# Two loads for w1's first rows, first FFN products on four banks, packed turns of q: one change to a fused attention and FFN kernel

## The chip, the core and the metric

The kernel runs on one core of a Trainium2 chip. The metric is the device time of one execution in microseconds (us); the text compares medians of several runs. A profile is one further execution, recorded by the hardware profiler, with its own time.

A core has five engines that run their own instruction queues in order and wait for each other through semaphores: PE (TensorE: matrix products, results into PSUM), DVE (VectorE), ACT (ScalarE), POOL (GpSimd, used here to issue loads that also convert fp32 to bf16) and SP (SyncE, used here to issue stores and transposing transfers). PSUM has eight banks of 512 fp32 columns by 128 partitions.

## What is computed

Linformer attention for 8 batches of 8 heads (1024 positions, head size 64), followed by a feed-forward layer (FFN) with a maximum over three products:

```python
k_proj = einsum('ks,bhsd->bhkd', E, k)            # 64 projected positions
v_proj = einsum('ks,bhsd->bhkd', F, v)
scores = q @ k_proj^T / sqrt(64)
attn   = softmax(scores)
x      = (attn @ v_proj) -> 8192 tokens x 512
h      = max(x @ w1, x @ w2, x @ w3)              # 512 x 768 each
out    = h @ w_out                                # 768 x 512
```

## The kernel before

**Tiling.** A batch is a loop turn `b` of eight. Its 1024 tokens are two chunks `ch` of 512. The 512 model columns are four row blocks `ct` of the weights (128 rows each; one block of x is one pair of heads, `g` or "pair"), the 768 hidden columns six blocks `jt`. Everything multiplied is bf16.

**FFN.** `up_mm` (line 565) issues one 128x128 by 128x512 product for one weight `i`, one `jt` and one `ct`. For most chunks `up` (609) does the three weights of one `jt`, ACT copies the first result (625), DVE takes the maxima (629, and `most`, 577), then `down` (655) multiplies by `w_out` for four token tiles `tt`. Steps 0 to 5 of a chunk are the `jt`, steps 6 to 9 the `tt`.

**Attention for a batch** is woven between these steps: `kproj` and `vproj` (E and F against k and v, 341 to 351), `kt` (turn of the projected keys), `qd` (380: DVE packs q into `q_p` head by head side by side, SP turns it with a transposing transfer), `sc` (321: scores; the exponentials on ACT are put off to the next `run_later` unless `now` is set), then sums and values. `za` (330) takes the sums of one pair with a matrix of ones, the values, and on ACT logarithm and exponential for the reciprocal (`invert`, 288), and DVE scales the values into `xT` (`scale_x`, 305). `zc` (248) does the sums of a whole chunk in a compact form: the reciprocals go to DRAM (`zd`, line 268, on SP) and come back spread over partitions (`zi_all`, four transfers, line 275, on SP or on the queue given).

**Order.** Everything is placed by hand. `plan(b)` (685) is a table: key `(ch, step)` gives what is issued after that step; `(1, (3, "mid"))` is in the middle of step 3. Queues keep the order of issue.

**PSUM banks** are dealt by the program when it is built. `two()` (77) gives an aligned pair and `bank()` (82) one bank; both take what is free earliest by the kernel's own arithmetic of when each engine gets there (`clock`, `free`; `at(us)` moves that arithmetic on). A bank dealt but not yet read out is marked open and isn't dealt again. If its former reader is later on the chip than assumed, PE waits.

**The start.** Loads for batch 0 are issued by POOL in lines 167 to 195: q, k and v by parts, w1's row blocks 0 and 1 as one load (185), v for pairs 2 and 3, w1's other blocks, w2, w3, the second half of q, w_out. The first chunk of batch 0 has its own attention, in lines 507 to 559: `v_pair(g)` projects v for a pair, `z(g)` does sums and reciprocals, `x(g)` values and scaling. `idle` issues products on a constant, whose results nobody reads. Then `up_first` (580) does the first FFN chunk: six banks for w1, `ct` outside and `jt` inside; `work` says what is issued after product `(0, ct, jt)`. After that, w2 and w3 (i = 1, 2) each run first with row blocks 0 and 1 (step "a"), then with 2 and 3, each followed by DVE's maximum. `qp` (363), issued within the w3 part, turns chunk two of q on PE: `heads_q` (353) turns one head of 64 columns at a time.

The next batch's q, k and v are loaded by `ld`; in batch 1's plan the loads of batch 3 stand at `(0, 3)` and `(0, 8)`.

Of the kernel before, what the change touches and what calls it, by code (L numbers as in the profile page):

```python
# [15 lines left out]
def kernel(  # L16
# [60 lines left out]
    def two():  # L77
        n = min(range(0, 8, 2), key=lambda n: max(free[n:n + 2]))
        deal((n, n + 1))
        return psum_t[:, n:n + 2, :], (n, n + 1)  # L80
# [80 lines left out]
    def load_w(i, cts):  # L161
        w = (moe_w1, moe_w2, moe_w3)[i].rearrange("(ct p) j -> p ct j", p=P)
        nc.gpsimd.dma_start(out=w_sb[i][:, cts, :], in_=w[:, cts, :])
# [18 lines left out]
            at = hp * 16 + c * 8  # L182
            nc.vector.memset(pick[c * HALF:(c + 1) * HALF, hp, at:at + 8], 1.0)

    load_w(0, slice(0, 2))
    load_kv(2, V2)
    load_kv(2, V3)
    load_w(0, slice(2, 3))
# [132 lines left out]
    def sc(b, g, lo=0, nsi=SI, now=False):  # L321
        def f():
            t = scores(b, g, lo, nsi)
            if now:
                exps(b, g, lo, nsi, t)
            else:
                later.append(lambda: exps(b, g, lo, nsi, t))
        return f

    def za(b, g, lo=0, nsi=SI, then=False):  # L330
        def f():
            z = sums(b, g, lo, nsi)
            av = values(b, g, lo, nsi)
            invert(b, g, lo, nsi, z)
            if then:
                later.append(lambda: scale_x(b, g, lo, nsi, av))
            else:
                scale_x(b, g, lo, nsi, av)
        return f
# [13 lines left out]
    def heads_q(b, g, sis, t):  # L353
        for i, si in enumerate(sis):
            for hp in range(2):
                nc.tensor.transpose(
                    out=t[hp * HALF:(hp + 1) * HALF, i * P:(i + 1) * P],
                    in_=qkv[b][0][:, 2 * g + hp, si, :],
                    identity=ident,
                )  # L360
        pe(0.08 * len(sis))

    def qp(b, gs, lo=0, nsi=SI):
        def f():
            if b not in qTs:
                qTs[b] = att.tile([P, NPAIR * SI, P], BF16, name="qT")
            t, ns = two()
            t = t.bitcast(BF16)[:, 0]
            n = nsi * P
            for i, g in enumerate(gs):  # L370
                heads_q(b, g, range(lo, lo + nsi), t[:, i * n:(i + 1) * n])
            o = qTs[b].rearrange("a (g si) p -> a g si p", si=SI)
            copy(
                "v", o[:, gs[0]:gs[-1] + 1, lo:lo + nsi, :],
                t[:, 0:len(gs) * n].rearrange("a (g si p) -> a g si p", si=nsi, p=P),
                ns, 0.1 + len(gs) * nsi * 0.08,
            )
        return f
# [20 lines left out]
    def kproj(b):  # L399
        def f():  # L400
            t, ns = bank()
            proj(b, 1, t, (LO, HI), 4 * D)
            kps[b] = att.tile([P, 2, 2 * D], BF16, name="kp")
            copy("v", kps[b].rearrange("a g x -> a (g x)"), t[:, 0:4 * D], ns, 0.43)
        return f
# [31 lines left out]
    def idle(n, w=warm):  # L437

        t, ns = bank()
        for _ in range(n):  # L440
            nc.tensor.matmul(out=t, lhsT=w[:, 0:P], rhs=w, start=True, stop=True)  # L441
        free[ns[0]] = pe(n * MM * (4 if w is warm_f else 1))
# [19 lines left out]
    def at(us):  # L462
        clock["pe"] = max(clock["pe"], us)
# [56 lines left out]
    def z(g):  # L520
        invert(0, g, *C0, sums(0, g, *C0))

    def x(g):
        scale_x(0, g, *C0, values(0, g, *C0))
# [28 lines left out]
        exps(0, g, *C0, scores(0, g, *C0))  # L553
    at(16.1)
    v_pair(1)
    idle(1)
    x(1)
    z(2)
    z(3)
    at(18.2)  # L560

    ffn_sb = ctx.enter_context(tc.tile_pool(name="ffn_sb", bufs=2))
    hTs = {}
# [16 lines left out]
    def up_first(work):  # L580


        def then(key):
            run_later()
            for f in work.get(key, []):
                f()

        hs = ffn_sb.tile([P, NJT, CHUNK], FP32, name="hs", bufs=1)
        hTs[0, 0] = ffn_sb.tile([P, NJT, CHUNK], BF16, name="hT")
        jts = range(NJT)  # L590
        h = [(t[:, n], ns[n:n + 1]) for t, ns in (two(), two(), two()) for n in (0, 1)]
        for ct in range(NCT):
            for jt in jts:
                up_mm(h[jt][0], 0, 0, 0, jt, (ct,))
                if ct == NCT - 1:
                    copy("sv"[jt % 2], hs[:, jt], *h[jt])
                then((0, ct, jt))
        for i in (1, 2):
            h = []
            for jt in jts:  # L600
                h.append(bank())
                up_mm(h[jt][0], i, 0, 0, jt, range(NCT // 2))
                then((i, "a", jt))
            for jt in jts:
                up_mm(h[jt][0], i, 0, 0, jt, range(NCT // 2, NCT))
                most(hs[:, jt] if i == 1 else hTs[0, 0][:, jt, :], *h[jt], hs[:, jt])
                then((i, jt))
# [74 lines left out]
    def ld(b, which=(0, 1, 2)):  # L682
        return lambda: load(b, which)

    def plan(b):
        n = b + 1
        if b == 0:
            c1 = (SPC, SPC)
            return {
                (0, 6): [za(0, 1, *c1), sc(0, 3, *c1)],  # L690
                (0, 7): [qd(1, 2), za(0, 2, *c1)],
                (0, 8): [za(0, 3, *c1)],
                (1, 0): [kproj(1)],
                (1, 1): [kt(1)],
                (1, 2): [vproj(1), ld(2)],
                (1, (3, "mid")): [sc(1, 0), sc(1, 1)],
                (1, 4): [za(1, 0), sc(1, 2)],
                (1, 5): [za(1, 1), sc(1, 3)],
                (1, 7): [za(1, 2)],
                (1, 8): [za(1, 3)],  # L700
            }
        if b == 1:
            return {
                (0, 0): [qd(2)],
                (0, 3): [kproj(2), vproj(2), ld(3, (0, 1))],
                (0, 4): [kt(2)],
                (0, 5): [sc(2, 0, now=True), sc(2, 1, now=True), sc(2, 2)],
                (0, 6): [sc(2, 3)],
                (0, 8): [zc(2, nc.gpsimd), ld(3, (2,))],
                (1, 1): [qd(3)],  # L710
                (1, 3): [vx(2, 0), vx(2, 1)],
                (1, 6): [vx(2, 2), vx(2, 3)],
            }
        if b == 2:
            return {
                (0, 1): [kproj(3), vproj(3), ld(4)],
                (0, 2): [kt(3)],
                (0, 3): [sc(3, 0, now=True), sc(3, 1)],
                (0, 5): [sc(3, 2, now=True), sc(3, 3)],
                (0, 7): [zc(3)],  # L720
                (0, 8): [qd(4)],
                (1, 3): [kproj(4), vproj(4), ld(5), vx(3, 0), vx(3, 1)],
                (1, 4): [kt(4)],
                (1, 6): [vx(3, 2), vx(3, 3), sc(4, 0)],
            }
        if n == B:
            return {}
        out = {
            (0, 1): [sc(n, 1, now=True), sc(n, 2, now=True), sc(n, 3)],
            (0, 3): [zc(n)],  # L730
            (1, 2): [vx(n, 0), vx(n, 1)],
            (1, 6): [vx(n, 2), vx(n, 3)],
        }
        if n + 1 < B:
            out[0, 4] = [qd(n + 1)]
            out[1, 2] = [kproj(n + 1), vproj(n + 1)] + out[1, 2]
            out[1, 3] = [kt(n + 1)]
            out[1, 6] += [sc(n + 1, 0)]
        if n + 2 < B:
            out[1, 3] += [ld(n + 2)]  # L740
        return out

    for b in range(B):
        p = plan(b)

        def behind(ch, step):
            for f in p.get((ch, step), []):
                f()

        for ch in range(NCHUNK):  # L750
            if (b, ch) == (0, 0):
                c1 = (SPC, SPC)
                up_first({
                    (0, 0, 5): [lambda: v_pair(2)],
                    (0, 1, 2): [lambda: x(2)],
                    (0, 1, 5): [lambda: v_pair(3), ld(1)],
                    (0, 2, 2): [lambda: x(3)],
                    (2, "a", 2): [qp(0, (0, 1), *c1)],
                    (2, "a", 4): [qp(0, (2, 3), *c1)],
                    (2, 0): [sc(0, 0, *c1)],  # L760
                    (2, 2): [sc(0, 1, *c1)],
                    (2, 4): [za(0, 0, *c1, then=True), sc(0, 2, *c1)],
                })
                run_later()
                behind(0, NJT - 1)
            else:
                for step in range(NJT):
                    up(b, ch, step, lambda: behind(ch, (step, "mid")))
                    behind(ch, step)
            for tt in range(SPC):  # L770
                down(b, ch, tt, "v" if b == 0 else "s")
                behind(ch, NJT + tt)
# [30 lines left out]
```

The softmax here doesn't subtract the row's maximum and nothing guards it: scores larger than these inputs give would overflow.

## Time and profile before

| | |
|---|---|
| median of 11 runs | 402.79 us (402.06 to 404.31) |
| the profiled execution: time, span | 403.11 us, 401.3 us |
| PE busy | 392.0 us (98%), 2303 products |
| DVE busy | 202.9 us (51%) |
| ACT busy | 149.0 us (37%) |
| POOL busy | 34.1 us (8%) |
| DMA | 66.11 MB, mean 165 GB/s |
| FFN products with w1, w2, w3 | 1152 |
| products with w_out | 378 |

The profiled execution took 1.8 us more than its span; all places in time below are counted from the span's start. "Busy" of PE includes the pipelining of products, so a stall on PE shows better as a distance between the starts of two neighbours than as missing busy time. In a timeline line, the columns are start, length, engine, source line, operation, written tile <- read tiles, form, count, and in brackets the idle time of the engine just before with what ended it. Lines of copies carry L102, the helper's.

### The profile page before, as it was taken

How to read it: one execution, taken by the hardware profiler on the slowest of the kernel's cores; microseconds unless marked ns; L12 is line 12 of the kernel's file. 1: busy time of each engine (PE TensorE's matmuls, PEld its weight loads, DVE VectorE, ACT ScalarE, POOL GpSimd, SP SyncE). 2: the span in 40 equal slices, each digit the busy share in tenths (PEclk: the TensorE clock that was granted, in tenths of full speed). 3: DMA queues.
4: the chain of work that ended last, by engine and by line, in shares of the span. 5: the costliest groups of instructions: out<-in, count | busy, mean ns of one | idle time of the engine just before them, and what ended most of it. 6: DMA issues, size and time to landing. Idle time of an engine off the chain costs nothing.

```text
span 401.3 us, 5779 instructions
## 1 busy us (share of the span) xinstructions
PE 392.0 (98%) x2303; PEld 176.4 (44%) x2303; DVE 202.9 (51%) x319; ACT 149.0 (37%) x238; POOL 34.1 (8%) x48
## 2 busy tenths in 40 slices
PE   7899999999999999999999999999999999999996
PEld 3444444353435435444454445444454444444443
DVE  2338755761664525826274544744267342745251
ACT  2621537527213452253323532245323533132322
POOL 7340002010301000200020000200000000000000
PEclk9999999999999999999999999999999999999999
DMA  8999999979799988999899949993890229020202
GB/s 146 206 206 207 232 212 154 238 140 184 225 175 257 186 181 197 176 222 194 193 233 177 240 118 198 223 238 70 198 222 2 105 64 253 2 106 0 105 2 105
DMA packets 66316, 66.11 MB, mean 165 GB/s; under 512 B 30609, under 2 KB 58769, under 8 KB 66289
## 3 DMA queue, kind: packets, MB, share of 16 engines
q0 software_dynamic: 29088, 30.41, 47.0%
q1 hardware_dynamic: 37056, 35.20, 35.0%
q8 instruction: 18, 0.29, 0.3%
q10 hardware_dynamic: 144, 0.13, 0.1%
q14 instruction: 10, 0.07, 0.1%
HBM read 69.73 MB, written 16.97 MB: 216 GB/s over the span
## 4 chain that ended last, share of the span: by engine, by line
PE 84%; DMA 6%; DVE 3%; ACT 2%; issue 2%; POOL 1%; DVEq 0%; POOLq 0%; ACTq 0%
PE banks L567 56%; PE banks L664 19%; DMA w_sb<-in_moe_w_dram 3%; PE banks L345 3%; PE banks L231 2%; PE banks L211 2%; DMA zi_all<-zd 2%; DVE xT L308 2%; DMA zd<-zic 1%; PE banks L256 1%; ACT zl L291 1%; ACT zi_all L297 1%; DVE m L629 1%; DVE hT L577 0%; POOL k_t L152 0%
## 5 line engine op out<-in xcount | busy, mean ns | idle before, releaser
L567 PE MATMUL banks<-xT,w_sb 128*128 128x512 bf16 x1152 | 257.6, 380 | 1.5 <-DMA w_sb<-in_moe_w_dram 1.2
L567 PEld LDWEIGHTS <-w_sb 128*128 128x128 bf16 x1152 | 109.9, 98 | 137.8 <-issue 8.7
L629 DVE TENSOR_TENSOR m<-banks,h1s 128x512 f32<-128x512 f32 x90 | 62.1, 690 | 135.9 <-ACT h1s L625 92.4
L625 ACT COPY h1s<-banks 128x512 f32<-128x512 f32 x90 | 52.6, 585 | 119.7 <-PE banks L567 117.6
L664 PE MATMUL banks<-wout_sb,hT 128*128 128x512 bf16 x378 | 87.1, 380 | 1.0 <-DVE hT L577 1.0
L577 DVE TENSOR_TENSOR hT<-banks,m 128x512 bf16<-128x512 f32 x90 | 62.3, 692 | 10.4 <-PE banks L567 0.8
L664 PEld LDWEIGHTS <-hT 128*128 128x128 bf16 x378 | 35.3, 98 | 49.1 <-issue 5.8
L102 ACT COPY o_sb<-banks 128x512 f32<-128x512 f32 (+1 forms) x56 | 32.6, 582 | 58.9 <-PE banks L664 58.6
L222 ACT ACTIVATE pT<-banks 128x1024 bf16<-128x1024 f32 (+1 forms) x36 | 32.7, 932 | 25.9 <-PE banks L211 25.9
L308 DVE TENSOR_TENSOR xT<-banks,zi_all 128x1024 bf16<-128x1024 f32 x28 | 33.2, 1220 | 12.3 <-PE banks L231 5.5
L200 POOL DMA_DIRECT2D q_t<-in_q_dram x7 | 6.1, 877 | 193.7 <-DMA qT<-q_p 66.5
L102 DVE CAST vp<-banks 64x256 bf16<-64x256 f32 (+1 forms) x18 | 7.1, 397 | 12.1 <-ACT vp L102 8.4
L345 PEld LDWEIGHTS <-efT 128*64 128x64 bf16 x224 | 11.6, 110 | 3.4 <-issue 3.0
L102 ACT CAST vp<-banks 64x256 bf16<-64x256 f32 x14 | 5.1, 364 | 20.3 <-PE banks L345 20.2
L231 PE MATMUL banks<-pT,vp 64*64 64x512 bf16 (+1 forms) x144 | 11.5, 364 | 0.4 <-DVE vp L102 0.4
L211 PE MATMUL banks<-qT,kpT 64*64 64x512 bf16 (+1 forms) x144 | 11.2, 362 | 0.0
L291 ACT ACTIVATE zl<-banks 128x512 f32<-128x512 f32 (+1 forms) x12 | 8.9, 739 | 5.2 <-PE banks L231 4.4
L102 DVE COPY q_p<-q_t 128x1024 bf16<-128x1024 bf16 x28 | 10.0, 420 | 0.0
L102 DVE COPY o_sb<-banks 128x512 f32<-128x512 f32 (+1 forms) x9 | 5.8, 654 | 4.5 <-PE banks L644 4.5
L441 PE MATMUL banks<-warm_f 128*128 128x512 f32 x8 | 6.1, 903 | 1.5 <-DVE warm_f L175 1.5
L345 PE MATMUL banks<-k_t,efT 128*64 128x256 bf16 x112 | 7.5, 276 | 0.0
L345 PE MATMUL banks<-v_t,efT 128*64 128x256 bf16 x112 | 7.3, 273 | 0.0
(60 smaller groups left out, 119.0 us busy)
## 6 DMA issues: line engine op xcount, KB each, us to landing
out_dram<-o_sb SPq DMA_DIRECT2D x30, 512.0 KB, 4.6
zi_all<-zd SPq DMA_DIRECT2D x20, 512.0 KB, 7.7
q_t<-in_q_dram POOLq DMA_DIRECT2D x7, 1024.0 KB, 9.5
k_t<-in_k_dram POOLq DMA_DIRECT2D x7, 1024.0 KB, 15.5
v_t<-in_v_dram POOLq DMA_DIRECT2D x7, 1024.0 KB, 21.2
zi_all<-zd POOLq DMA_DIRECT2D x4, 512.0 KB, 8.1
w_sb<-in_moe_w_dram POOLq DMA_DIRECT2D x5, 384.0 KB, 12.4
k_t<-in_k_dram POOLq DMA_DIRECT2D x2, 512.0 KB, 9.1
```

The source lines that it names most:

```text
L102: done = {"v": nc.vector.tensor_copy, "s": nc.scalar.copy, "g": nc.gpsimd.tensor_copy}[eng](out=o, in_=i)
L211: nc.tensor.matmul(out=t[c * HALF:(c + 1) * HALF, hp, 0:n * P], lhsT=kpTs[b][rows, g, :], rhs=qTs[b][rows, at:at + n, :], start=True, stop ...
L222: nc.scalar.activation(out=pTs[b, g, lo], in_=t, func=AF.Exp, scale=scale)
L231: nc.tensor.matmul(out=t[hp * HALF:(hp + 1) * HALF, c, 0:nsi * HALF], lhsT=w(rows, hp), rhs=p[rows, hp, :], start=True, stop=True,)
L291: nc.scalar.activation(out=zl, in_=t, func=AF.Ln)
L308: nc.vector.tensor_tensor(out=xTs[b][:, g, lo:lo + nsi, :].rearrange("a (c s) p -> a c (s p)", c=2), in0=t, in1=zi, op=ALU.mult,)
L345: nc.tensor.matmul(out=t[hh * HALF:(hh + 1) * HALF, 0:width], lhsT=efT[:, si, (kv - 1) * KP:kv * KP], rhs=qkv[b][kv][:, heads[hh], si, :], ...
L567: nc.tensor.matmul(out=h, lhsT=w_sb[i][:, ct, jt * P:(jt + 1) * P], rhs=xTs[b][:, ct, ch * SPC:(ch + 1) * SPC, :], start=(ct == first), st ...
L577: nc.vector.tensor_tensor(out=o, in0=h, in1=other, op=ALU.max)
L625: nc.scalar.copy(out=h1s, in_=h[0][0])
L629: nc.vector.tensor_tensor(out=m12, in0=h[1][0], in1=h1s, op=ALU.max)
L664: nc.tensor.matmul(out=o_ps, lhsT=hTs[b, ch][:, jt, tt * P:(tt + 1) * P], rhs=wout_sb[:, jt, :], start=(jt == 0), stop=(jt == NJT - 1),)
```

## The change

- Line 185's load of w1's row blocks 0 and 1 becomes two loads.
- Before `up_first`: `idle(1)`, `x(1)`, `z(2)`, `z(3)` are no longer there; `x(1)` now comes after product (0, 0, 1) and both sums after (0, 0, 3).
- `up_first` deals w1's banks when they are needed, and orders the products: `ct` 0 and 1 for `jt` 0 to 3, then `ct` 0 and 1 for `jt` 4 and 5, then `ct` 2 and 3 for all six. Value projections and value products of pairs 2 and 3 move as in the diff.
- Chunk two of q: DVE packs two heads side by side (`pack_q`, two copies of 128x512 for two pairs, after w3's steps "a" 0 and "a" 1), and PE turns 128 columns at once.
- Batch 0's plan at (1, 4): scores of pair 2 ahead of sums and values of pair 0.
- Batch 1's plan: the load of k for batch 3 moves from (0, 3) to (0, 8), behind the reciprocals' transfers, which there are on POOL's queue.

```diff
-    load_w(0, slice(0, 2))
+    load_w(0, slice(0, 1))
+    load_w(0, slice(1, 2))
...
+    def pack_q(b, gs, lo, nsi):
+        def f():
+            if b not in q_pk:
+                q_pk[b] = att.tile([P, NPAIR, SI, 2, D], BF16, name="q_p", bufs=1)
+            for g in gs:
+                copy(
+                    "v", q_pk[b][:, g, lo:lo + nsi].rearrange("p si h d -> p h si d"),
+                    qkv[b][0][:, 2 * g:2 * g + 2, lo:lo + nsi], (), 0.25,
+                )
+        return f
...
-                heads_q(b, g, range(lo, lo + nsi), t[:, i * n:(i + 1) * n])
+                for si in range(nsi):
+                    nc.tensor.transpose(
+                        out=t[:, i * n + si * P:i * n + (si + 1) * P],
+                        in_=q_pk[b][:, g, lo + si].rearrange("p h d -> p (h d)"),
+                        identity=ident,
+                    )
+                pe(0.06 * nsi)
...
     v_pair(1)
-    idle(1)
-    x(1)
-    z(2)
-    z(3)
-    at(18.2)
+    at(17.4)
...
-        h = [(t[:, n], ns[n:n + 1]) for t, ns in (two(), two(), two()) for n in (0, 1)]
-        for ct in range(NCT):
-            for jt in jts:
+        h = {}
+        for ct, js in (
+            (0, range(0, 4)), (1, range(0, 4)), (0, range(4, 6)), (1, range(4, 6)),
+            (2, jts), (3, jts),
+        ):
+            for jt in js:
+                if jt not in h:
+                    t, ns = two()
+                    for n in (0, 1):
+                        h[jt + n] = t[:, n], ns[n:n + 1]
...
-                (1, 4): [za(1, 0), sc(1, 2)],
+                (1, 4): [sc(1, 2), za(1, 0)],
...
-                (0, 3): [kproj(2), vproj(2), ld(3, (0, 1))],
+                (0, 3): [kproj(2), vproj(2), ld(3, (0,))],
...
-                (0, 8): [zc(2, nc.gpsimd), ld(3, (2,))],
+                (0, 8): [zc(2, nc.gpsimd), ld(3, (1, 2))],
...
-                    (0, 0, 5): [lambda: v_pair(2)],
-                    (0, 1, 2): [lambda: x(2)],
-                    (0, 1, 5): [lambda: v_pair(3), ld(1)],
+                    (0, 0, 1): [lambda: x(1)],
+                    (0, 0, 3): [lambda: z(2), lambda: z(3)],
+                    (0, 1, 3): [lambda: v_pair(2)],
+                    (0, 1, 5): [lambda: x(2), lambda: v_pair(3), ld(1)],
                     (0, 2, 2): [lambda: x(3)],
+                    (2, "a", 0): [pack_q(0, (0, 1), *c1)],
+                    (2, "a", 1): [pack_q(0, (2, 3), *c1)],
```

More of the change, by code (lines that the diff above doesn't have):

```diff
@@ L361, in heads_q, with qp @@
         pe(0.08 * len(sis))
-    def qp(b, gs, lo=0, nsi=SI):
+    q_pk = {}
+    def pack_q(b, gs, lo, nsi):
         def f():
-            if b not in qTs:
-                qTs[b] = att.tile([P, NPAIR * SI, P], BF16, name="qT")
+            if b not in q_pk:
[6 more added lines that the diff above has]
+        return f
+    def qp(b, gs, lo, nsi):
+        def f():
             t, ns = two()
```

## The prediction, on record before the changed kernel ran

> **What bounds the kernel now.** I read the waits of PE over the whole run first:
>
> ```profile
> PE banks L441 <- DVE warm_f L175: 1.5, 1, 1.5
> PE banks L567 <- DMA w_sb<-in_moe_w_dram: 1.2, 1, 1.2
> PE banks L470 <- DMA k_t<-in_k_dram: 1.1, 1, 1.1
> PE banks L664 <- DVE hT L577: 1.0, 1, 1.0
> ...
> PE banks L231 <- DVE xT L308: 0.3, 1, 0.3
> ```
>
> Columns: us in total, times, longest. PE, 98% busy on the page, is the bound, and few holes are left. The change touches three: the 1.2 us before the first FFN product, 1.0 before a `w_out` product, 0.3 before a sums product. Starts of neighbours say what each costs: two FFN products start 0.216 us apart, product to attention product 0.309. At these holes the distances are 1.47, 1.34 and 0.73 us.
>
> Next the timeline of the start and of the places that the edits touch:
>
> ```profile
> 16.92 0.69 DVE L308 TENSOR_TENSOR xT<-banks,zi 128x512 bf16<-128x512 f32 x1 [0.35 <-PE banks L231]
> ...
> 16.97 0.62 PE L496 MATMUL banks<-v_t,efT 128*128 128x128 bf16 x8
> ...
> 17.98 0.30 PE L231 MATMUL banks<-pT,vp 64*64 64x256 bf16 x4 [0.17 <-DVE vp L102]
> ...
> 18.11 0.39 PE L231 MATMUL banks<-pT,ones 64*64 64x256 bf16 x8
> 18.40 0.69 DVE L308 TENSOR_TENSOR xT<-banks,zi 128x512 bf16<-128x512 f32 x1 [0.48 <-PE banks L231]
> ...
> 30.23 3.68 DVE L577 TENSOR_TENSOR hs<-banks,hs 128x512 f32<-128x512 f32 x6 [2.07 <-PE banks L567]
> ...
> 33.51 0.64 PE L356 MATMUL banks<-ident,q_t 128*64 128x128 bf16 x16
> ...
> 56.04 0.80 PEld L345 LDWEIGHTS <-efT 128*64 128x64 bf16 x16 [0.43 <-DMA v_t<-in_v_dram]
> ```
>
> See three things. DVE ends w2's maxima at 33.91, after PE has already turned the first q at 33.51. Chunk-two q costs PE 0.57 us per sixteen turns. And the weights for batch 1's v projection at 56.04 were released by v's landing at 55.92: v has no slack there. The chain of waits begins `6.39 13.26 DMA`: w1's first load lands at 19.66. Its landing events show fifteen of the sixteen engines done by 18.39; the last is 1.27 us later, behind a 16 KB packet of the instruction queue that starts at 17.64 and takes 0.97 us.
>
> **The start: about +0.05 us.** Two loads of w1 blocks 2 and 3, of the half size, land 0.92 us apart (22.59, 23.51); so the first half should be done some 0.95 us before the fifteen engines' 18.39, at 17.45, ahead of the instruction packet. The Trainium skill, "DMA: Bandwidth & Descriptors", section "Rules for kernel authors", speaks against the split: transfers of 1 MiB and more, and under "Anatomy of one DMA" a fixed 2.0 us for each. If the queue paid that, an estimate from the page would be everything behind up to 2 us later and 405 us at the end; the 0.92 us between those neighbours leaves no room for it.
>
> `xT` of pair 0 ends at 17.61, so the first product can start at 17.67 instead of 19.70. What follows, with distances from the trace (product to value product 0.31, those four and back 0.23, projection 0.45, product to DVE start 0.42): two products, `x(1)` at 18.20, DVE 18.62 to 19.31; two products; `z(2)` at 18.95. The open pairs hold four banks; `z(2)` takes one free pair, and by the dealing `z(3)` gets that of `x(1)`, so it waits to 19.37. Its logarithm comes after `z(2)`'s two on ACT (0.60, 0.63), and ends at 21.18. Row block 1 starts at 19.70, when its load lands; four products; `v_pair(2)` at 20.58 to 21.02. Products of `jt` 4 get `z(3)`'s pair: wait to 21.24. Four products, `x(2)` at 22.20, DVE to 23.29. Now six banks are open and `x(2)` holds the last two: `v_pair(3)`, next in PE's queue, **waits 0.8 us for DVE**, to 23.35. Before, `x(2)` had three products behind it, and `v_pair(3)` began at 23.30. Then three products, `x(3)` at 24.53, DVE to 25.64, row block 3 at 25.70. Before: 25.65. The 2 us of earlier start are spent on sums that had lain in the wait (0.5), and on four bank waits. Bounds: −0.1, if row block 1 lands early too; +1.1, if the first half also lands at 18.7.
>
> **Packed turns: +0.87.** PE gains nothing: sixteen half-width turns start 28 ns apart, full-width ones (L412, L452) 56 to 64, and there are eight; at most 0.03 us per group. DVE gets four copies of 512 columns. A copy of that size within SBUF took 0.28 us (efT, at 8.57), the packing of 1024 columns 0.42 and 0.355 start to start; so two take 0.50. They queue behind w2's maxima, which end at 33.91: the first pair of copies is done at 34.34, PE can turn at 34.40, where it now turns at 33.51. PE's products of `jt` 3 are behind the waiting turns. Wait 0.89, less 0.02. The second copies end near 34.85, before the second turns at 35.9. Bounds: 0.75 with copies at the half of 0.355, 1.0 with 0.28 each without overlap. Nothing between 34 and 56 takes it back: PE has no hole over 0.06 there. If the start should be faster, DVE's maxima move with PE and the wait stays.
>
> **The order at (1, 4): +0.23.** Four scores (0.23 us on PE) now precede sums of pair 0 at 62.99. Logarithm, exponential and scaling follow the sums, and the scaling frees the bank that `za(1, 1)` gets, in either order. So the hole at 66.87 grows. Scores gain nothing: their exponential is put off to the same place on ACT. Bounds: −0.42 (the hole goes, if another pair is dealt) to +0.25.
>
> **k of batch 3: −0.7.** The `w_out` hole:
>
> ```profile
> 113.00 2.36 DVE L308 TENSOR_TENSOR xT<-banks,zi_all 128x1024 bf16<-128x1024 f32 x2 [1.97 <-DMA zi_all<-zd]
> ...
> 118.20 0.39 PE L664 MATMUL banks<-wout_sb,hT 128*128 128x512 bf16 x1 [0.96 <-DVE hT L577]
> ```
>
> DVE waits for the reciprocals' second transfer (landed 112.88), falls behind, and PE pays 1.34 − 0.22 = 1.12 us. That transfer waits for `zd`, issued at 99.86 and landed at 104.42, 4.56 us, beside the load of k (landed 104.24) and a store; with an idle queue `zd` takes 1.8 (232.40 and later). Without k, `zd` should land near 101.8, POOL issue at 102.3 and the second `zi_all` land at 110.2, before DVE is free at 111.03. DVE gains the 1.97, PE 1.12.
>
> Then k and v queue behind 2 MB of `zi_all` (9.3 us, from 103.3 to 112.6), beside the q transpose from about 113, where a load got 150 KB/us in 119 to 124. 2 MB at that rate is 13.7 us, plus some 1.7 as lost in 115 to 119: v lands at about 128.2, where it landed at 124.95. PE wants it at 129.05, or 128.0 with the hole gone. So some 0.4 us may come back as a wait at `vproj(3)`; between none (−1.12) and 2 us (+0.9). k at 121 is in time. The transpose ends some 2 us later (130), the scores that need it come at 134.4; the next loads have over 6 us of slack.
>
> **Sum.** 0.05 + 0.87 + 0.23 − 0.7 = +0.45. The profiled execution took 403.11, so 403.56; it lies 0.32 above the median of 402.79, so **403.2** against that. Up to 0.2% (0.8 us) is no change that a measurement of this kernel can tell.
>
> **Rivals.**
>
> *The early products pay (15%).* If bank waits and packing cost less than I think, PE could be at 56 us up to 1.5 us earlier. But v of batch 1 lands at 55.92 behind a DMA queue that has been full since 3 us, whose bytes don't change. So nothing over 0.1 us survives `vproj(1)`. The most is −0.1, −1.12 from k and nothing from (1, 4): −1.2, 401.6; halfway 402.0. For it: PE work alone from 17.67 to row block 3 is only 6.3 us. Against: bank dealing and DVE's order.
>
> *v of batch 3 is late (20%).* Slower: if `vproj(3)` waits over 1.12 us, the edit costs. It decides when v lands after 129.1. For it: 2 MB more in line at 112; against: the idle DMA queue from 97 to 103. With a landing at 129.5, +0.4 from k and +1.15 from the others: 404.3.
>
> *The first half lands no earlier (12%)*, because the instruction packet meets it, or it is held by the same slow engine: first product at 18.74, all as above a microsecond later, since x(1), sums and banks follow in chain: +1.05, 404.3.
>
> *The forecast (53%)*: 402.3 to 404.0.
>
> **Chances.** Faster by over 0.2% (under 402.0): most of half of the first rival and a corner of the forecast, 0.13. Slower (over 403.6): the two slow rivals and a part of the forecast's upper half: 0.37. Within: 0.50. Range 401.9 to 404.6: it leaves out the best corner of the k edit, and a late v on top of a late first half.
>
> **What would show it.** After: first FFN product near 17.7, a PE wait of 0.8 us before `v_pair(3)` on DVE's xT, row block 3 still near 25.7; a wait of 0.9 us before the first turns on DVE's q_p; the hole of `za(1, 1)` at 0.6; no hole before the `w_out` product of chunk two in batch 1, but perhaps one before `vproj(3)` on v. It is wrong if turns start without a wait, if row block 3 starts before 25, or if v of batch 3 is over a microsecond off 128.

## The result and the profile after

The changed kernel takes 404.40 us in the median of 15 runs (403.67 to 405.40), the kernel before 402.89 (55 runs, on the same chips). The ratio is 1.0037, 95% interval 1.0028 to 1.0045: slower by some 1.5 us. The profiled execution took 403.98 us with a span of 402.2, 0.9 us longer than the one before; single executions differ by more than a microsecond, so the medians carry the verdict and the traces the places.

The six largest of PE's nine waits over the run, changed kernel (helper lines have moved: L212 scores, L232 sums and values, L386 turns, L516 v's projection in the start, L583 FFN, L687 `w_out`):

```profile
PE banks L461 <- DVE warm_f L175: 1.5, 1, 1.5
PE banks L212 <- DMA qT<-q_p: 0.9, 1, 0.9
PE banks L516 <- DVE xT L309: 0.9, 1, 0.9
PE banks L490 <- DMA k_t<-in_k_dram: 0.9, 1, 0.9
PE banks L386 <- DVE q_p L102: 0.6, 1, 0.6
PE banks L232 <- DVE xT L309: 0.6, 1, 0.6
```

Two entries of before are gone: the 1.2 us for w1's load and the 1.0 before a `w_out` product. Four are new or larger: 0.9 before v's projection, 0.6 before the turns, 0.6 (from 0.3) before sums, and the one in the second line that the forecast doesn't have, 0.9 before scores that wait for a transposing transfer of q.

The same places in the timeline of the changed kernel:

```profile
17.78 0.59 PE L583 MATMUL banks<-xT,w_sb 128*128 128x512 bf16 x2 [0.17 <-DVE xT L309]
...
22.38 0.30 PE L232 MATMUL banks<-pT,vp 64*64 64x256 bf16 x4
...
23.55 0.61 PE L516 MATMUL banks<-v_t,efT 128*128 128x128 bf16 x8 [0.86 <-DVE xT L309]
...
34.09 0.89 DVE L102 COPY q_p<-q_t 128x512 bf16<-128x512 bf16 x4
...
34.43 0.62 PE L386 MATMUL banks<-ident,q_p 128*128 128x128 bf16 x8 [0.59 <-DVE q_p L102]
...
67.73 0.41 PE L232 MATMUL banks<-pT,ones 64*64 64x512 bf16 x4 [0.56 <-DVE xT L309]
...
116.84 1.46 PE L687 MATMUL banks<-wout_sb,hT 128*128 128x512 bf16 x6
...
169.21 0.41 PE L212 MATMUL banks<-qT,kpT 64*64 64x512 bf16 x4 [0.95 <-DMA qT<-q_p]
```

The first product starts at 17.78 and not at 19.70, but the values of pair 2 (22.38) and v's projection behind them (23.55) stand 1.17 us apart, as forecast. The six `w_out` products at 116.84 now run without the hole. To see where time comes and goes, I laid the starts of the same FFN and `w_out` products of the two traces beside each other. The changed kernel stands

| up to | shift of the changed kernel | of it new |
|---|---|---|
| w1's row block 3 (25.91; before 25.65) | +0.26 | +0.26 |
| after the two groups of turns | +0.66 | +0.40 |
| after the hole near 67 | +0.86 | +0.20 |
| after the `w_out` hole near 118 | −0.28 | −1.14 |
| after the scores at 169.21 | +0.85 | +1.13 |

From there on it stays. So the gain of the k edit comes as forecast and is taken back whole, 51 us later.

### The profile page after: what moved, and what is told of

The parts are those of the page before. It is cut to its first block, busy times and chain, and to the rows that moved or that the text cites. A ratio compares the mean times of both kernels' runs of the same rounds, so it can differ in the third digit from the quotient of the medians.

```text
span 402.2 us, 5751 instructions
## 1 busy us (share of the span) xinstructions
PE 392.5 (98%) x2286; PEld 176.8 (44%) x2286; DVE 204.3 (51%) x323; ACT 149.0 (37%) x238; POOL 34.4 (9%) x49
## 4 chain that ended last, share of the span: by engine, by line
PE 88%; DMA 5%; ACT 2%; DVE 2%; issue 1%; POOL 0%; DVEq 0%; ACTq 0%; POOLq 0%
PE banks L583 58%; PE banks L687 19%; DMA qT<-q_p 4%; PE banks L346 3%; PE banks L232 2%; PE banks L212 2%; DMA k_t<-in_k_dram 2%; ACT zl L292 1%; DVE xT L309 1%; PE banks L257 1%; ACT zi_all L298 1%; DVE hs L593 1%; PE banks L490 1%; PE banks L461 0%; PE banks L667 0%
## 5 line engine op out<-in xcount | busy, mean ns | idle before, releaser
L583 PE MATMUL banks<-xT,w_sb 128*128 128x512 bf16 x1152 | 257.7, 380 | 0.7 <-DVE xT L309 0.3
L583 PEld LDWEIGHTS <-w_sb 128*128 128x128 bf16 x1152 | 110.0, 98 | 136.6 <-issue 9.0
L687 PE MATMUL banks<-wout_sb,hT 128*128 128x512 bf16 x378 | 86.9, 380 | 0.1
L687 PEld LDWEIGHTS <-hT 128*128 128x128 bf16 x378 | 35.3, 98 | 47.6 <-issue 5.6
L212 PE MATMUL banks<-qT,kpT 64*64 64x512 bf16 (+1 forms) x144 | 11.2, 363 | 0.9 <-DMA qT<-q_p 0.9
L232 PE MATMUL banks<-pT,vp 64*64 64x512 bf16 (+1 forms) x144 | 11.4, 364 | 0.3 <-DVE vp L102 0.2
L102 DVE COPY q_p<-q_t 128x1024 bf16<-128x1024 bf16 (+1 forms) x32 | 11.3, 418 | 0.0
L309 DVE TENSOR_TENSOR xT<-banks,zi 128x512 bf16<-128x512 f32 x8 | 5.5, 690 | 3.9 <-PE banks L232 3.0
## 6 DMA issues: line engine op xcount, KB each, us to landing
w_sb<-in_moe_w_dram POOLq DMA_DIRECT2D x4, 384.0 KB, 10.9
```

The costliest lines, as they stand in the source:

```text
L102: done = {"v": nc.vector.tensor_copy, "s": nc.scalar.copy, "g": nc.gpsimd.tensor_copy}[eng](out=o, in_=i)
L212: nc.tensor.matmul(out=t[c * HALF:(c + 1) * HALF, hp, 0:n * P], lhsT=kpTs[b][rows, g, :], rhs=qTs[b][rows, at:at + n, :], start=True, stop ...
L232: nc.tensor.matmul(out=t[hp * HALF:(hp + 1) * HALF, c, 0:nsi * HALF], lhsT=w(rows, hp), rhs=p[rows, hp, :], start=True, stop=True,)
L309: nc.vector.tensor_tensor(out=xTs[b][:, g, lo:lo + nsi, :].rearrange("a (c s) p -> a c (s p)", c=2), in0=t, in1=zi, op=ALU.mult,)
L583: nc.tensor.matmul(out=h, lhsT=w_sb[i][:, ct, jt * P:(jt + 1) * P], rhs=xTs[b][:, ct, ch * SPC:(ch + 1) * SPC, :], start=(ct == first), st ...
L687: nc.tensor.matmul(out=o_ps, lhsT=hTs[b, ch][:, jt, tt * P:(tt + 1) * P], rhs=wout_sb[:, jt, :], start=(jt == 0), stop=(jt == NJT - 1),)
```

## Experiments

**Theory A**, from this table and from the DMA packets: the wait near 169 has two parents. Batch 4's q is turned by a transfer behind the reciprocals of batch 3 on SP's queue, and these move beside a chain of loads that the k edit made later: v of batch 4 landed at 148.94 before and at 153.13 now, `zd` at 150.41 and 152.14 (3.52 and 5.54 us after its issue), the q transpose at 167.38 and 169.16. And packing has taken 16 products off PE (the start one more). The instruction queue moves packets of 16 KB. I take them for fetches of PE's instructions: there are 18 in the run before for 2303 products and as many weight loads, one per 256 of them, and with 17 products fewer the second one starts at 38.32 and not at 35.71. With fewer products, then, each fetch meets other neighbours. Before, one started at 161.9; now it starts at 164.4, inside the q transpose. **Theory B**: the fetches don't matter, and the later loads alone make the wait. **The forecast's sizes** (0.05, 0.87, 0.23, −0.7) are the third candidate.

### Each part undone

```diff
 a_noK: the load of k back at (0, 3)
-                (0, 3): [kproj(2), vproj(2), ld(3, (0,))],
+                (0, 3): [kproj(2), vproj(2), ld(3, (0, 1))],
-                (0, 8): [zc(2, nc.gpsimd), ld(3, (1, 2))],
+                (0, 8): [zc(2, nc.gpsimd), ld(3, (2,))],
 a_noQ: half-width turns, no packing
-                for si in range(nsi):
-                    nc.tensor.transpose(
...
+                heads_q(b, g, range(lo, lo + nsi), t[:, i * n:(i + 1) * n])
-                    (2, "a", 0): [pack_q(0, (0, 1), *c1)],
-                    (2, "a", 1): [pack_q(0, (2, 3), *c1)],
 a_noW: the order at (1, 4) as before
-                (1, 4): [sc(1, 2), za(1, 0)],
+                (1, 4): [za(1, 0), sc(1, 2)],
 a_noS: load_w(0, slice(0, 2)) in one, and the old order of x(1), z(2), z(3) and of the products
```

a_noK: 

> The changed kernel with k of batch 3 loaded where it was before, at (0, 3). Theory (from the two traces): the edit gives PE 1.14 us at the w_out product of batch 1's second chunk and takes 1.13 back in batch 2, where the first scores of batch 4 wait for the transpose of q, late behind a chain of later loads. Undone, the hole near 118 returns, the wait near 169 goes, and the time stays within 0.3 us of the changed kernel's 404.4. Rival (the forecast's size): the edit is worth 0.7 us, so undoing it gives about 405.1. Second rival: the 1.5 us between the medians, of which the traces show 0.9, contain 0.6 us that k and v of batch 3 cost in most executions; then undoing gives about 403.8.

a_noQ: 

> The changed kernel with chunk two of q turned by half-width turns straight from q, with no packing on DVE. Theory (from the traces): the first group of turns waits 0.59 us for DVE, the second group gets 0.15 back; without it 0.40 us less, 404.0. Rival (the forecast's size): 0.87 us less, 403.5. Rival that full-width turns save PE time: no change or slower than 404.4.

a_noW: 

> The changed kernel with sums and values of pair 0 ahead of the scores of pair 2 again at (1, 4) of batch 0. Theory: the wait before the sums of pair 1 shrinks from 0.56 to 0.35 us and the time by 0.2 us, to 404.2. Rival: the order is worth nothing or gains, because the wait is only moved; 404.4 or more.

a_noS: 

> The changed kernel with the start as before: one load for w1's row blocks 0 and 1, sums and values ahead of the first FFN product, six banks at once. Theory (from the traces): row block 3 starts 0.26 us later in the changed kernel in spite of a first product 1.92 us earlier; undone, 404.1. Rival (the forecast): +0.05, so 404.35. Rival that the early products pay: slower than 404.4 by up to the 0.7 us by which v of batch 1 lands earlier.

| kernel | median us (runs) | before, same chip | ratio (95%) | against 1.0037 |
|---|---|---|---|---|
| a_noK | 403.10 (12) | 402.36 | 1.0021 (1.0011 to 1.0031) | −0.0016, 0.6 us |
| a_noQ | 402.50 (11) | 402.36 | 1.0003 (0.9995 to 1.0012) | −0.0034, 1.4 us |
| a_noW | 404.04 (5) | 402.36 | 1.0041 (1.0029 to 1.0053) | +0.0004 |
| a_noS | 403.77 (5) | 402.36 | 1.0040 (1.0028 to 1.0052) | +0.0003 |

Nearly all of the loss goes when packing goes, more than three times what the first trace shows for it (0.40). The k edit is worth −1.14 us in one place and costs 0.6 in sum. Each difference to 1.0037 is itself known only to ±0.0013 to ±0.0016 (0.5 to 0.6 us), so that of a_noK is just clear of noise. The misses: a_noK was expected within 0.3 us of 404.4 and is faster; a_noQ is faster than both of its numbers. The order at (1, 4) and the start change nothing that 0.12% can tell. PE's waits in a_noQ over the whole run, the four largest of seven (the others are 0.4 us or less, and none is for q):

```profile
PE banks L455 <- DVE warm_f L175: 1.5, 1, 1.5
PE banks L510 <- DVE xT L309: 0.9, 1, 0.9
PE banks L484 <- DMA k_t<-in_k_dram: 0.8, 1, 0.8
PE banks L232 <- DVE xT L309: 0.6, 1, 0.6
```

The wait for `qT<-q_p` isn't there, although k's load still stands behind the reciprocals. So the k edit alone doesn't make it; this speaks for A.

### Product count, the waits themselves, and k alone

```diff
 a_pad: 17 small products in the start's wait for k (results unread), in the changed kernel
-    idle(1, warm_f)
+    idle(1, warm_f, 17)
...
+        for _ in range(small):
+            nc.tensor.matmul(
+                out=t[:, 0:HALF], lhsT=warm[:, 0:P], rhs=warm[:, 0:HALF], start=True, stop=True
+            )
 a_sc: scores of batch 4 two steps later, in the changed kernel
-                (1, 6): [vx(3, 2), vx(3, 3), sc(4, 0)],
+                (1, 6): [vx(3, 2), vx(3, 3)],
+                (1, 8): [sc(4, 0)],
 a_Qlate: turns one step later, in the changed kernel
-                    (2, "a", 2): [qp(0, (0, 1), *c1)],
-                    (2, "a", 4): [qp(0, (2, 3), *c1)],
+                    (2, "a", 3): [qp(0, (0, 1), *c1)],
+                    (2, "a", 5): [qp(0, (2, 3), *c1)],
 b_K: in the kernel before, the k edit alone
```

a_pad: 

> The changed kernel with 17 more small products (64 columns, on a constant) in the start's wait for k, before 10 us, where PE idles. The changed kernel has 17 products fewer on PE than before (16 turns, one idle product), so that PE's later fetches of instructions fall at other places. Theory A: packing costs 1.4 us, 0.4 for DVE's wait and about 1.0 because a 16 KB fetch of PE's instructions now falls into the q transpose of batch 4 and holds it, so the scores of batch 4 wait near 169; with the old count of products that wait goes: ratio 1.0012 to 1.0015 to the kernel before. Rival B: the wait comes from the later chain of loads alone and the fetches don't matter: 1.0037 as the changed kernel, with the wait near 169.

a_sc: 

> The changed kernel with the first scores of batch 4 two steps later, at (1, 8) of batch 2 instead of (1, 6); nothing is left out. Theory: the wait near 169 for the transpose of q of batch 4 is real time on PE, about 1 us; here the transpose has 2.7 us more, the wait goes, ratio 1.0014. Rival: the wait is covered by a later one (the loads that follow), 1.0037.

a_Qlate: 

> The changed kernel with both groups of q turns one step later (after (2, a, 3) and (2, a, 5)). Theory A: the wait of 0.59 us for DVE before the turns goes, the wait near 169 stays, 0.4 to 0.6 us less: ratio 1.0024. Rival: all of the 1.4 us that packing costs is this wait and what follows from it: 1.0003.

b_K: 

> The kernel before with one edit: k of batch 3 loaded behind the reciprocals. Theory A: the hole of 1.1 us before the w_out product near 118 goes, no new wait comes, since PE's instruction fetches stay where they were: ratio 0.9975. Rival B: the later chain of loads makes the scores of batch 4 wait whatever the fetches do: 1.0000 (forecast of the record for this edit alone, with 0.4 us given back at v of batch 3: 0.9983).

| kernel | median us (runs) | before, same chip | ratio (95%) | against 1.0037 |
|---|---|---|---|---|
| a_pad | 403.29 (12) | 402.88 | 1.0007 (0.9996 to 1.0018) | −0.0030, 1.2 us |
| a_sc | 403.26 (11) | 402.88 | 1.0009 (0.9996 to 1.0022) | −0.0028, 1.1 us |
| a_Qlate | 403.84 (11) | 402.88 | 1.0024 (1.0015 to 1.0034) | −0.0013, 0.5 us |
| b_K | 402.45 (12) | 402.88 | 0.9983 (0.9971 to 0.9996) | |

**A kernel with 17 useless products more is 1.2 us faster.** B is out. Up to the place near 169 the two go alike: from row block 3 to behind the `w_out` hole, a_pad and the changed kernel both gain 0.54 us on the kernel before. There the changed kernel loses 1.13 and a_pad 0.15, since its q lands at 168.40, just as PE arrives (PE's timeline, a_pad):

```profile
166.23 1.71 PE L691 MATMUL banks<-wout_sb,hT 128*128 128x512 bf16 x6
167.87 0.63 PE L232 MATMUL banks<-pT,vp 64*64 64x512 bf16 x8
168.44 0.41 PE L212 MATMUL banks<-qT,kpT 64*64 64x512 bf16 x4
```

And the DMA of the stretch in which the transpose's data moves, changed kernel: GB/s in 40 slices of 0.155 us, packets by queue, and the transposes that were in progress (queue q8 is the instruction queue; the last number is us from issue to landing):

```profile
GB/s 264 89 185 155 175 197 182 102 40 21 286 388 273 273 140 0 0 0 7 8 8 10 10 175 291 291 291 291 291 291 287 291 291 291 284 291 291 291 287 462
...
q8 instruction: 1, 0.02, 1.1%
...
qT<-q_p SPq DMA_TRANSPOSE x1, 14.2
```

and a_pad, where the fetch starts at 161.9, ahead of the transpose's first packet at 162.6 (slices of 0.1375 us):

```profile
GB/s 93 246 128 164 162 227 147 186 99 41 56 26 56 41 19 117 289 289 290 289 294 289 290 289 292 290 290 287 294 289 292 287 290 292 292 285 292 287 595 484
...
qT<-q_p SPq DMA_TRANSPOSE x1, 13.5
```

In both, the queue slows for about a microsecond. In a_pad that is from 163.7 to 164.6, while the last reciprocals are still on their way (landed 164.85); in the changed kernel they had landed at 164.34, and it is the transpose itself that comes to a stop, at 164.9, half a microsecond after the fetch began. From issue to landing it takes 14.2 us against 13.5, and 0.7 us decides, because PE arrives when it lands. All profiled kernels that have these scores at the old place, one trace each:

| kernel | products on PE | k behind the reciprocals | fetch starts | last reciprocals to q landed, us | wait before scores of batch 4, us |
|---|---|---|---|---|---|
| changed | 2286 | yes | 164.40 | 4.82 | 0.95 |
| a_noW | 2286 | yes | 164.10 | 4.84 | 1.08 |
| a_Qlate | 2286 | yes | 163.85 | 4.80 | 0.70 |
| a_x2 (below) | 2286 | yes | 163.40 | 4.83 | 0.67 |
| a_noS | 2287 | yes | 163.85 | 4.83 | 0.74 |
| a_noQ | 2302 | yes | 161.17 | 3.53 | none |
| a_pad | 2303 | yes | 161.90 | 3.55 | none over 0.15 |
| b_K | 2303 | yes | 160.40 | 3.53 | none |
| a_noK | 2286 | no | 163.67 | 4.75 | none |
| before | 2303 | no | 161.90 | 4.91 | none |
| b_split (below) | 2303 | no | 161.58 | 4.92 | none |

In these eleven kernels both conditions go with the wait, and neither alone does. The fifth column says how. Where the fetch runs past the landing of the last reciprocals, the transpose needs 4.75 to 4.92 us more; where it has ended by then, 3.53 to 3.55, and the last reciprocals have taken some 0.6 us longer in its place (10.5 to 10.9 us from issue to landing against 9.9 to 10.4). The three kernels with later scores fall on the same two values (a_sc 4.80, b_best 3.53, a_fix 3.54). So the kernel before, whose fetch starts at 161.90 as in a_pad, has its transpose stopped too; but its chain is earlier (last reciprocals at 162.47, not 164.85), and q lands 1.0 us before PE wants it. It takes the later chain and the fetch inside the transpose to make PE wait. That is why undoing one of two parts each gives more than its share, and why the k edit is −0.0017 alone and +0.0016 in company.

a_sc shows that the wait is real time: 1.1 us come back by the medians when the scores stand later, and in its trace 0.23 us are left of the 1.13.

a_Qlate came out at its number, but not for its reason. Turning later only moves packing's wait to the scores that need the turned q, as its waits say:

```profile
PE banks L212 <- DVE qT L102: 0.3, 1, 0.3
...
PE banks L386 <- DVE q_p L102: 0.2, 1, 0.2
```

From row block 3 to behind these scores it loses 0.38 us on the kernel before, where the changed kernel loses 0.40. Of the 0.5 us that its median is better (known to about ±0.5), the trace accounts for 0.25, the shorter wait near 169; the rest isn't explained. So packing's own cost, 0.40, rests on the traces: the shift is 0.38 to 0.40 in every kernel that packs and none in a_noQ.

### The start, and what could be had

```diff
 a_x2: the values of pair 2 two products earlier, in the changed kernel
+                    (0, 0, 5): [lambda: x(2)],
-                    (0, 1, 5): [lambda: x(2), lambda: v_pair(3), ld(1)],
+                    (0, 1, 5): [lambda: v_pair(3), ld(1)],
 b_split: in the kernel before, the split load alone
 b_best: in the kernel before, the split load, the k edit and the later scores of a_sc
 a_fix: the changed kernel with a_noQ, a_noW, a_x2 and the later scores of a_sc
```

a_x2: 

> The changed kernel with the values of pair 2 issued two products earlier, after product (0, 0, 5), so that the products (0, 1, 4) and (0, 1, 5) stand between them and v's projection for pair 3. Theory: the 0.87 us that this projection waits for DVE to read the last two banks is what eats the early start; 0.4 to 0.65 us of it goes, ratio 1.0022 to 1.0027 (the wait near 169 stays). Rival: another of the chain's waits (reciprocals on ACT, v's landing) takes its place, 1.0037.

b_split: 

> The kernel before with w1's row blocks 0 and 1 as two loads and nothing else. Theory: the first half lands near 17.5, the first product starts near 18.5 instead of 19.7, about 0.75 us are left at row block 3, and v of batch 1 (landed 55.25 to 55.9) lets 0.1 to 0.75 us through: ratio 0.9982 to 0.9997. Rival from the forecast: v's landing lets nothing through, 1.0000.

b_best: 

> The kernel before with three edits: w1's first row blocks as two loads, k of batch 3 behind the reciprocals, the first scores of batch 4 two steps later. Theory: the gains of the k edit (0.7 us) and of the split add: ratio 0.9965 to 0.998. Rival: v of batch 1 and of batch 3 land too late for the earlier PE, and no more than the k edit's 0.9983 is left, or less.

a_fix: 

> The changed kernel with its new start and load of k, the values of pair 2 two products earlier, half-width turns without packing, the old order at (1, 4), and the first scores of batch 4 two steps later. Theory: start 0.2 to 0.4 us better than before, k 0.7 us: ratio 0.9973 to 0.998. Rival: the new start stays no better than the old one, 0.9983 or above.

| kernel | median us (runs) | before, same chip | ratio (95%) |
|---|---|---|---|
| a_x2 | 403.33 (12) | 402.98 | 1.0011 (1.0001 to 1.0021) |
| b_split | 402.71 (12) | 402.98 | 0.9990 (0.9980 to 1.0000) |
| b_best | 402.45 (11) | 402.98 | 0.9986 (0.9977 to 0.9996) |
| a_fix | 402.48 (11) | 402.98 | 0.9985 (0.9975 to 0.9995) |

Since the first microseconds differ between executions, the start is read as a distance: from the first value product of `x(0)` (16.49 before) to the first product of row block 3.

| kernel | start of it | us |
|---|---|---|
| before | old order, one load | 9.16 |
| a_noS | old order, one load, landed at 18.85 | 8.57 |
| b_split | old order, two loads | 8.57 |
| b_best | old order, two loads | 8.80 |
| changed | new order, two loads | 9.39 |
| a_x2 | new order, values of pair 2 earlier | 8.96 |

The split gains 0.6 us here with the old order (0.36 in b_best); the new order loses 0.8, more than that gain, of which a_x2 gives 0.43 back. PE's start in a_x2, where the wait before v's projection is 0.33 instead of 0.86:

```profile
21.45 0.30 PE L232 MATMUL banks<-pT,vp 64*64 64x256 bf16 x4
21.68 0.60 PE L583 MATMUL banks<-xT,w_sb 128*128 128x512 bf16 x2
22.62 0.61 PE L516 MATMUL banks<-v_t,efT 128*128 128x128 bf16 x8 [0.33 <-DVE xT L309]
```

By the medians a_x2 is 0.0026, 1.05 us, better than the changed kernel, more than twice the 0.43 that the trace accounts for. Some of the rest may be a shorter wait near 169 (0.67 in its profiled execution); beyond that it isn't explained. In a_noS the old single load landed at 18.85 and not at 19.66. Its fetch of instructions came at 18.0 and not at 17.6, which may be the reason and isn't shown. So a_noS undoes more than the edit, and doesn't size it.

Where the gain of the split goes is seen in b_split, timeline of PE:

```profile
54.81 0.38 PE L568 MATMUL banks<-xT,w_sb 128*128 128x512 bf16 x1
56.20 1.06 PE L346 MATMUL banks<-v_t,efT 128*64 128x256 bf16 x16 [1.01 <-DMA v_t<-in_v_dram]
```

PE is early by 0.9 us and waits 1.0 for v of batch 1, which landed at 56.15. What this execution keeps at its end, 0.4 us, comes from a smaller `w_out` hole later (0.42 instead of 0.96). a_fix waits there 0.5 us, and 0.56 more for v of batch 3:

```profile
128.53 0.74 PE L346 MATMUL banks<-v_t,efT 128*64 128x256 bf16 x10 [0.56 <-DMA v_t<-in_v_dram]
```

So three rather different kernels (b_K, b_best, a_fix) end at 0.9983 to 0.9986, beside each other within their intervals: the rivals' outcome in b_best and a_fix, whose forecast sums were too good, though both intervals still reach them. b_K, the smallest edit, is as good as any.

## Why the prediction came out as it did

The measured 404.40 lies in the range (401.9 to 404.6), at its upper end. But the likeliest case, within 0.2%, didn't happen; slower did, which had 0.37. That the number stayed in the range is in part luck: the upper end was drawn for a late v or a late first half of w1, neither of which came, and what filled it was a wait of 1.1 us that the forecast doesn't have. Step by step, against "0.05 + 0.87 + 0.23 − 0.7":

- **The start, +0.05: nearly right.** Trace: +0.23 in distance. First product 17.78 (forecast 17.67), wait before v's projection 0.86 (0.8), row block 3 at 25.91 (25.70). The first half landed at 17.48 (17.45), the second 0.92 later, and the next load of w1 no later than before (22.46 and 22.59), so the split cost the queue nothing. The forecast of row block 3 is 0.2 short; waits come where it puts them. That this costs time beside the old order is only seen in the trace: undone, the median stays within 0.12%.
- **Packed turns, "+0.87": mis-sized, and one step failed.** DVE's copies wait for the maxima and PE for the copies, as forecast. The shift after the first group grew by 0.55, not 0.87. The turns waited for the first copy only, not for "the first pair of copies": the copies start 0.20 apart from 34.09 and take 0.29 each, and PE turns at 34.43, when the second still runs. And each group saves PE 0.11 to 0.13 us, where I had "at most 0.03 us per group": from its first turn to the next product a group takes 0.44 to 0.46 instead of 0.57. The sum is 0.40 in the trace. The step that failed is "PE gains nothing", and with it the sum, which has no term for the number of products: sixteen fewer move the fetches of instructions. That makes most of the rest of what undoing packing gives back (1.4 by a_noQ; a_pad, which keeps packing, gives back 1.2).
- **The order at (1, 4), +0.23: right in the trace** (+0.20; the wait grew from 0.35 to 0.56, in a_noW it is 0.35 again). The medians can't tell it: a_noW's 1.0041 has an interval of ±0.0012.
- **k of batch 3, −0.7: mechanism right, the give-back at the wrong place.** `zd` took 1.82 us (forecast: lands near 101.8; it did at 102.54, with PE 0.9 later), the hole of 1.12 went and PE gained 1.14. v landed at 128.72, PE's v projection began at 128.85, 0.13 us after: the forecast had 128.2 and 0.4 us of wait, "between none and 2"; none came. In place of it came 1.13 us at the scores of batch 4. The step that failed is "the next loads have over 6 us of slack". They have, at their own readers. But on their way they hold up `zd` and, behind it on SP's queue, the q transpose of batch 4, which had 1.0 us (landed 167.38, scores at 168.39). Alone, on b_K, the edit is worth −0.0017, 0.7 us (0.2 to 1.2). That is the forecast's number, but not its sum: b_K's trace gains 1.15 us and gives nothing back at v.
- **Rivals.** "Nothing over 0.1 us survives `vproj(1)`" is borne out by the waits of b_split and a_fix, where PE does get there early; in the changed kernel PE is late and v's landing doesn't matter. "v of batch 3 is late" happened in a_fix (0.56 us), not here. "The first half lands no earlier" didn't happen.

The sum of the trace is 0.23 + 0.40 + 0.20 − 1.14 + 1.13 = 0.82 us; the medians are 1.51 apart. Of the 0.69 between, the two profiled executions account for 0.64: the one before lies 0.22 above its median, the one after 0.42 below. Which waits differ in those executions stays open.

## What to carry to other kernels

When a load is moved later, follow not only its own reader but every transfer that it will stand beside or that waits in the same queue, down to the one with the least slack; here that was a transpose 60 us on. In a start that is bound by banks, issuing products earlier only pays if the instruction behind a pair's last reader has something else to do: two products between the values and the next projection were worth 0.43 us. And before a fully busy DMA queue, gains on PE end at the next load that has no slack.

## What the runs showed of the hardware

- **The number of PE instructions can change the time by more than the instructions themselves.** The instruction queue moved 18 packets of 16 KB in the run before. Beside one of them (17.64) the last share of w1's load landed 1.27 us after the other fifteen; beside another a transposing transfer of q stopped in mid-flow (changed kernel, 164.9). In all fourteen traces this transpose lands 4.75 to 4.92 us after the last reciprocals when a fetch runs past their landing, and 3.53 to 3.55 when it has ended. Moving the fetches by 17 small products in a place where PE idles anyway took 1.2 us off the changed kernel (a_pad against it, 1.0007 to 1.0037). Why a fetch stops the transpose is not shown.
- **A load beside a transposing transfer is slower than beside none**: in the changed kernel k and v of batch 3 came at about 150 KB/us from 115 to 127, where the queue gives about 200 alone (40 to 47 in the trace of before). In the microsecond from 118, after a fetch of instructions at 117.4, the loads fell to 62 KB/us and the transpose from about 39 to 16.
- **Full-width turns saved PE 0.11 to 0.13 us in a group of 0.57**, and not by their pace: eight of them start 56 ns apart where sixteen half-width ones start 28 ns apart. But the next product starts 0.06 us after the last full-width turn and 0.15 after the last half-width one (before, 35.46 to 35.62; changed, 36.22 to 36.28).
